# Transposing the features of two head pairs together, so that the w_in rows load in natural order

## The chip, the cores and the metric

The kernel runs on one core of one Trainium2 chip. The metric is the time of one execution in microseconds (us), as the median of several runs; shorter is better. The profile is of one such execution. Its span is about 2 us shorter than the timed value (212.5 against 214.5 us before). A run counts as slow when it is over 1.5% above the fastest run of the same kernel. The ratios, and the times that the text compares, are of the fast runs alone.

## The reference

Sliding-window attention (8 batches, 8 heads, 576 tokens, head size 64, window 32 each way), followed by a gated state-space layer. Cut to what matters:

```python
x    = attention(q, k, v)               # x[b, t, head * 64 + d]: the heads in order, 512 features
proj = x @ w_in                         # w_in: 512 x 1024
val, gate = proj[..., :512], proj[..., 512:]
for t in range(S):                      # a scan over the tokens
    h = exp(A_log) * h + val[:, t];  ys[:, t] = h
out  = (gate * sigmoid(gate) * ys) @ w_out
```

Any order of the 512 features between attention and projection is right, as long as the rows of `w_in` are in the same order.

## The kernel before

Tokens go in 9 chunks of 512 (8 blocks of 64). For each chunk and each of 4 head pairs TensorE (PE) makes scores (`sc`), ScalarE (ACT) the exponentials (`exp`), PE the product with v (`pv`), VectorE (DVE) the normalized result (`norm`) in 16 bit, and PE transposes it (`xt`), so that features lie on partitions; an eviction (`xe`) copies it from PSUM, where PE writes its results, to SBUF, from where it reads. Then come the projections (`pjv`, `pjg`), scan, gate, and output product (`fin`). Every engine follows an order written down in the kernel, one letter for each operation, and every load goes through the queue of the sync engine in the order of a list `ORDER`.

A head pair is heads 4G+s and 4G+2+s, because q and k are loaded in that arrangement. So each 128 features that come out of the transpose belong to two blocks of 64 rows of `w_in` that lie 128 rows apart. The load of `w_in` picks them:

```python
SLOTS = {..., "x16": 3, "xT": 2, ...}
        # loads
        elif kd == "ld" and key[0] == "a":
            nc.sync.dma_start(out=a_log, in_=moe_A_log.rearrange("(a p) -> p a", p=128))
            nc.scalar.activation(a1, a_log, AF.Exp, bias=0.0, scale=1.0)      # ACT, at the place of the load
        elif kd == "ld":
            _, i, a = key
            if i == 2:
                src = moe_w_out[128 * a:128 * a + 128, :]
            else:
                src = moe_w_in.rearrange("(g y s d) c -> g s y d c", g=2, y=2, s=2)[a // 2, a % 2, :, :, 512 * i:512 * i + 512]
            nc.sync.dma_start(out=bf("w32", i, a), in_=src)                   # 128 x 512 f32, 256 KB
        # ... (cut)
        elif kd == "cw":                                                      # cast to 16 bit
            i, a = key
            # ... (cut: w_out)
            copy(e, w_in16[:, a, 512 * i:512 * i + 512], bf("w32", i, a))
        # ... (cut)
        elif kd == "xt":                       # 4 transposes into free columns of the pv pair of banks
            x, pv = bf("x16", *key), bf("pv", *key)
            for half in range(2):
                dst = pv[:, half, 260:388].bitcast(f16)
                for r in range(2):
                    nc.tensor.transpose(out=dst[:, 128 * r:128 * r + 128],
                                        in_=x[:, 2 * half + r].rearrange("p h d -> p (h d)"), identity=ident)
        elif kd == "xe":                       # 36 evictions of 128 x 512
            c, hp = key
            copy(e, bf("xT", c)[:, hp, :].rearrange("p (a t) -> p a t", a=2),
                 bf("pv", *key)[:, :, 260:388].bitcast(f16))
```

The softmax here doesn't subtract the row's maximum and nothing guards it: scores larger than these inputs give would overflow.

Of the kernel before, what the change touches and what calls it, by code (L numbers as in the profile page):

```python
# [7 lines left out]
f32 = mybir.dt.float32  # L8
f16 = mybir.dt.float16
# [7 lines left out]

COST = {
    ("pe", "tr"): (0.50, 0.70), ("pe", "sc"): (0.235, 0.45), ("pe", "scm"): (0.455, 0.67), ("pe", "pv"): (0.265, 0.47),
    ("pe", "xt"): (0.23, 0.43), ("pe", "pj"): (0.864, 1.07), ("pe", "fin"): (0.864, 1.07),  # L20
    ("act", "ev"): (1.05, 1.20), ("act", "exp"): (0.92, 1.07), ("act", "tanh"): (0.50, 0.65),
    ("act", "fev"): (0.50, 0.65), ("act", "cv"): (0.53, 0.68), ("act", "cw"): (0.53, 0.68),
    ("act", "xe"): (0.50, 0.65), ("act", "sh"): (1.84, 1.99),
    ("dve", "ev"): (1.27, 1.40), ("dve", "mask"): (0.62, 0.74), ("dve", "rc"): (0.23, 0.25),
    ("dve", "norm"): (0.61, 0.74), ("dve", "xe"): (0.34, 0.47), ("dve", "scan"): (1.19, 1.33),
    ("dve", "silu"): (0.59, 0.72), ("dve", "cqk"): (0.66, 0.79),
    ("dve", "cv"): (0.34, 0.46), ("dve", "cw"): (0.34, 0.47), ("dve", "sh"): (0.62, 0.75),
    ("dve", "ar"): (0.65, 0.75), ("dve", "fuse"): (0.60, 0.72),
# [7 lines left out]
SWITCH, CAP, DLAT, DPRE = 0.095, 4.0, 0.95, 0.8  # L36
PEMASK = set(range(36))
SLOTS = {"stg": 5, "q16": 2, "k16": 2, "qT": 5, "kT": 5, "v32": 2, "vE": 2, "vO": 2, "pr": 3,
         "rc": 2, "x16": 3, "xT": 2, "f2k": 16, "th": 3, "si": 3, "fu": 2}
LETTER = {"L": "ld", "w": "cw", "a": "ar", "k": "ck", "K": "trk", "E": "evk", "q": "cq", "Q": "trq",  # L40
          "e": "evq", "v": "cv", "h": "sh", "S": "sc", "x": "exp", "P": "pv", "r": "rc", "n":
          "norm", "t": "xt", "T": "xe", "V": "pjv", "G": "pjg", "s": "scan", "g": "tanh", "u":
          "silu", "f": "fuse", "F": "fin", "o": "fev", "O": "out"}

SEQ = {
    "pe": "QQKSKSSPSPPPttQttKVVGSSGQVKVGSSPPPtPtGtQtKVGVVSSGQPPGtGKtVFSSFKPPFFttQKVGQQVSSSVGFKG"
          "PPSVttFSPPFGttQKFVVQGFSSSFPPGtVPPtGtFQGtVKQKVVSSKGQFSSPGFtKVKFPPPFtGtGtSSSVQGSPPGtFt"
          "VPPFGVKtFtGQVSSSFVGPPSGtVtSSPFVPPtVGtFGSSVFFtGFFPPPGtFtGVVVtVFGGVFVGVVFGGFFFFFFF",
    "act": "EvxvExxxwTTTTwgxgxeEvvgxxTTvTgeEghxxewggwwTgoxxEoooeEgexxxvgoEgxTTovxovgoeegoxxoxgTT"
           "ogvgeEEexxvgeoxxgoEEovoggxxxegxgoogToTexgxxogxTgTxxoTgoxgoxogooggooggogggoooooooo",  # L50
    "dve": "aqqeevvvhhrnrrwnrnneEsaususshhurnrnrnrnTsuuhssrnrTnuEusurrnnTTsuesshhurrnnusrrnnTTus"
           "EhuhsrnrnurnrTnsuTusssEhhurnTsurnrnTrnTTuhuhsrnrnuTTursnrunEsshuhsrnurnusrnrnssurTnu"
           "suTrrnnTurnTsuTssususssusuuf",
    "pool": "aakkqwkwwwwkqvfvvfqkfvvvvqfkfwfkfqkqqfvfvvvkfqkfqfqvvvfkkqffkqvvvfkkfvvqvvfqkffvfvvv"
            "fvfffffffffffff",
    "sp": "LLLLLLLLLLLLLLLLLLLLLLLLLLLLLLLLLLLLLLLLLLLLLLLLLLLLOLLLLLLLLLLLOOLLOLLLLLOLOLLLLOOL"
          "LLLLLLLOOOOLLOOOOOOOOOOOOOOOOOOOOOOOO",
}
SHARED = {
    "cw": "AGGDAGGGAAAG",  # L60
    "ar": "GDGD",
    "ck": "GGGGGGGGGGGGGGGG",
    "evk": "AADAADAAADAADAAD",
    "cq": "DDGGGGGGGGGGGGGG",
    "evq": "DDDAAAAADAAAAAAA",
    "cv": "DDAADGGGAAAGGGGGGAGGAAGGGAGAGGAGGGGGGGGG",
    "sh": "DDDDADDDDDDDDDDD",
    "xe": "AAAAAAADDADDAADDAADDDDDDDDAAAAADDDDD",
    "fuse": "GGGGGGGGGGGGGGGGGGGGGGGGGGGGGGGGGGGD",
}  # L70
ORDER = ["q01", "a", "v01", "q00", "v04", "k00", "v00", "v02", "k01", "v03", "w00", "w03",
         "q10", "k10", "w01", "w02", "w13", "w11", "w10", "w12", "k11", "q11", "v10", "v12",
         "v11", "v13", "v14", "k20", "q20", "v20", "v21", "v22", "v23", "v24", "q21", "w22",
         "k21", "w20", "w23", "w21", "k30", "q30", "k31", "q31", "v30", "q40", "v33", "v32",
         "v34", "v31", "k40", "v41", "v40", "q41", "k41", "q51", "v42", "q50", "k50", "v43",
         "k51", "v44", "v50", "q61", "q60", "v62", "v51", "k60", "v52", "v54", "v53", "k70",
         "v64", "k61", "v61", "v60", "v63", "v74", "q70", "v73", "q71", "v72", "k71", "v70",
         "v71"]
ORDER = [(x[0],) + tuple(int(y) for y in x[1:]) for x in ORDER]


# [8 lines left out]
def build(order):  # L90
# [3 lines left out]
    def add(kind, key, step, engs, cost, deps, new=(), use=()):  # L94
        o = Op()
        o.kind, o.key, o.engs, o.cost, o.deps = kind, key, engs, cost, [d for d in deps if d]
        o.new, o.use, o.step, o.n = list(new), list(use), step, len(ops)
        o.start = o.end = o.eng = None
        ops.append(o)
        last[(kind,) + key] = o  # L100
        return o
# [4 lines left out]
    g = last.get  # L106
    for it in order:
        if it[0] in "qk":
            add("ld", it, 0, ("sp",), 1.6, (), [("stg", it)])
        elif it[0] == "v":  # L110
            _, b, e = it
            add("ld", it, 0, ("sp",), 0.95 if e in (0, 4) else 1.24, (),
                [("v32", ("v32", b))])
        elif it[0] == "a":
            add("ld", it, 0, ("sp",), 0.8, ())
        else:
            add("ld", it, 0, ("sp",), 0.7, (), [("f2k", ("w32",) + it[1:])])
# [19 lines left out]
    for c in range(NCH):  # L137
        bs = sorted({(8 * c + r) // NBLK for r in range(8)})
        for hp in range(HP):
            k, st = (c, hp), 4 * c + hp  # L140
            s = add("sc", k, st, ("pe",), "scm" if st in PEMASK else "sc", [g(("ev" + n, b, hp // 2)) for n in "qk" for b in bs],
                    [("ps2", ("sc",) + k)], [(n + "T", b, hp // 2) for n in "qk" for b in bs])
            x = add("exp", k, st, ("act",), "exp", [s], [("pr", ("pr",) + k)], [("sc",) + k])
            m = x if st in PEMASK else add("mask", k, st, ("dve",), "mask", [x], (), [("pr",) + k])
            p = add("pv", k, st, ("pe",), "pv", [m] + [g(("cv", b, e)) for b in bs for e in range(5)] +
                    [g(("sh", b, i)) for b in bs for i in range(2)],
                    [("ps2", ("pv",) + k)], [("pr",) + k] + [(n, b) for n in ("vE", "vO") for b in bs])
            r = add("rc", k, st, ("dve",), "rc", [p], [("rc", ("rc",) + k)], [("pv",) + k])
            r = add("norm", k, st, ("dve",), "norm", [r], [("x16", ("x16",) + k)], [("pv",) + k, ("rc",) + k])
            t = add("xt", k, st, ("pe",), "xt", [r], (), [("x16",) + k, ("pv",) + k])  # L150
            add("xe", k, st, ("dve", "act"), "xe", [t], [("xT", ("xT", c))], [("pv",) + k])
    for c in range(NCH):
        xs = [g(("xe", c, hp)) for hp in range(HP)]
        for cc in range(4):
            k, st = (c, cc), 4 * c + cc
            pv = add("pjv", k, st, ("pe",), "pj", xs + [g(("cw", 0, a)) for a in range(4)],
# [121 lines left out]
def kernel(  # L278
# [18 lines left out]
    def T(shape, dt, tag):  # L297
# [2 lines left out]
    SHAPES = {"stg": ([128, 2, 9, 64], f32), "q16": ([128, 9, 2, 64], f16), "k16": ([128, 9, 2, 64], f16),  # L300
              "qT": ([128, 2, 576], f16), "kT": ([128, 2, 640], f16), "v32": ([128, 5, H, D], f32),
              "vE": ([128, 5, H, 65], f16), "vO": ([128, 4, H, 65], f16), "pr": ([128, 2, 512], f16),
              "rc": ([128, 4, 2], f32), "x16": ([128, 4, 2, 64], f16), "xT": ([128, HP, 512], f16),
              "f2k": ([128, 512], f32), "th": ([128, 512], f16), "si": ([128, 512], f16), "fu": ([128, 4, 512], f16)}
    bufs = {p: [T(SHAPES[p][0], SHAPES[p][1], f"{p}_{i}") for i in range(n)] for p, n in SLOTS.items() if p != "f2k"}
    f2k = T([128, SLOTS["f2k"], 512], f32, "f2k")
# [60 lines left out]
    def emit(o):  # L367
        e, key = o.eng, o.key

        def bf(*k):  # L370
            p, i = place[o.n, k]
            if p == "ps1":
                return psum[:, i, :]
            if p == "ps2":
                return psum[:, i:i + 2, :]
            return bufs[p][i]
# [16 lines left out]
        elif kd == "ld":  # L393
            _, i, a = key
            if i == 2:
                src = moe_w_out[128 * a:128 * a + 128, :]
            else:
                src = moe_w_in.rearrange("(g y s d) c -> g s y d c", g=2, y=2, s=2)[a // 2, a % 2, :, :, 512 * i:512 * i + 512]
            nc.sync.dma_start(out=bf("w32", i, a), in_=src)  # L399
        elif kd == "cw":  # L400
            i, a = key
# [70 lines left out]
            nc.vector.reciprocal(bf("rc", *key), view[:, :, :, 64])  # L472
        elif kd == "norm":
            view = bf("pv", *key)[:, :, 0:260].rearrange("p h (r x) -> p r h x", x=65)
            nc.vector.tensor_tensor(out=bf("x16", *key), in0=view[:, :, :, 0:64],  # L475
                                    in1=bf("rc", *key)[:, :, :, None].to_broadcast([128, 4, 2, 64]), op=ALU.mult)
        elif kd == "xt":
            x, pv = bf("x16", *key), bf("pv", *key)
            for half in range(2):
                dst = pv[:, half, 260:388].bitcast(f16)  # L480
                for r in range(2):
                    nc.tensor.transpose(out=dst[:, 128 * r:128 * r + 128],  # L482
                                        in_=x[:, 2 * half + r].rearrange("p h d -> p (h d)"), identity=ident)
        elif kd == "xe":
            c, hp = key
            copy(e, bf("xT", c)[:, hp, :].rearrange("p (a t) -> p a t", a=2),
                 bf("pv", *key)[:, :, 260:388].bitcast(f16))
        elif kd in ("pjv", "pjg"):
            c, cc = key
            oc = cc if kd == "pjv" else 4 + cc  # L490
# [63 lines left out]
```

## Time and profile before

| | before |
|---|---|
| time, median of all its runs in the first result | 214.59 us (212.74 to 215.18) |
| span of the profiled run | 212.5 us |
| PE busy | 162.1 us (76%) |
| DVE, ACT, POOL busy | 135.1, 120.8, 101.8 us |
| bytes moved by DMA | 41.22 MB |

The shares hide two stages. The table of stretches shows them. Its columns are: the stretch, its length, busy time and number of instructions of each engine, the granted PE clock, the DMA share (1.00 would be all 16 DMA engines busy; it adds up the times of packets, and can come out a little above 1), and GB/s.

```profile
core 0: us, PE busy (x) PEld busy (x) DVE busy (x) ACT busy (x) POOL busy (x), PEclk, DMA share, GB/s
20.00:30.00 10.00, 4.41 (x108) 3.56 (x104) 3.81 (x10) 3.73 (x5) 1.15 (x1) 0.84 0.30 99
30.00:40.00 10.00, 3.00 (x18) 1.59 (x17) 2.61 (x2) 1.08 (x2) 2.35 (x3) 0.50 0.13 51
40.00:50.00 10.00, 2.37 (x6) 0.60 (x4) 1.86 (x3) 0.00 (x0) 0.62 (x1) 0.50 0.13 51
50.00:60.00 10.00, 1.03 (x2) 0.13 (x2) 0.00 (x0) 0.63 (x1) 0.00 (x0) 0.50 0.73 193
61.00:209.00 148.00, 143.95 (x1872) 81.58 (x1872) 116.81 (x173) 108.11 (x151) 88.53 (x90) 0.99 0.75 218
```

From 30 to 50 us every engine is nearly idle, and so is DMA, at 0.13 of its engines: 2 of 16. From 61 us on PE is busy 97% of the time. What all wait for in between is in the chain of waits (start, length, what):

```profile
18.04 1.28 SPq L399
19.36 5.72 SPq L399
25.12 3.53 SPq L399
28.70 7.16 SPq L399
35.90 5.00 SPq L399
40.95 19.42 DMA f2k<-in_moe_w_in_dram
60.44 0.63 POOL w_in L358
61.11 1.19 PE psum L493 x2
```

SPq is the queue of the sync engine, L399 the issue of a weight load, L493 a projection. The queue is held by the issues of `w_in` loads, then the last of these takes 19.4 us to land, and only then the first full projection can end. The timeline of the sync engine has the `w_in` loads beside the loads of `w_out`, which have the same size and natural row order:

```profile
18.04 27.91 SPq L399 DMA_DIRECT2D f2k<-in_moe_w_in_dram  x6
...
76.72 1.41 SPq L399 DMA_DIRECT2D f2k<-in_moe_w_out_dram  x3
```

Six issues took 27.9 us here and three took 1.4 us there. The groups that the change touches (line, engine, operation, shapes, count, busy us, mean ns, idle time before and what ended it):

```profile
L482 PE MATMUL psum<-ident,x 128*128 128x128 f16 x144 | 14.0, 227 | 4.3 <-DVE x L475 4.2
L351 ACT ACTIVATE xT<-psum 128x512 f16<-128x512 f16 x17 | 9.9, 596 | 10.5 <-PE psum L482 10.2
L354 DVE COPY xT<-psum 128x512 f16<-128x512 f16 x19 | 7.7, 418 | 4.9 <-PE psum L482 4.8
```

### The profile page before, as it was taken

Reading aid. Unit: us, or ns where it says so; the run is one execution under the profiler, and the core shown is the slowest. Engines: PE = TensorE matmul, PEld = TensorE weight load, DVE = VectorE, ACT = ScalarE, POOL = GpSimd, SP = SyncE. Lnnn points to the kernel's source line nnn. Section 1 sums busy time; section 2 is a strip of 40 time slices with the busy share of each in tenths; the row PEclk is TensorE's granted clock in tenths of the full one; section 3 lists DMA queues with packets and bytes.
Section 4 is the critical chain, followed back from the end, with each engine's and each line's share of the span. In section 5 each row is a group of like instructions: output and inputs, shape, how many; then the busy total and the mean of one; then the engine's idle time right before and its main releaser. Section 6 shows DMA issues by size and latency. Waiting matters only on the chain.

```text
span 212.5 us, 5136 instructions
## 1 busy us (share of the span) xinstructions
PE 162.1 (76%) x2088; PEld 93.1 (44%) x2088; DVE 135.1 (64%) x218; ACT 120.8 (57%) x167; POOL 101.8 (48%) x115
## 2 busy tenths in 40 slices
PE   0258242500149798999999999899899999999993
PEld 0235132100025555576565566566555564554441
DVE  5463250500016969948876988958988977688950
ACT  2038330000118799888995959986737875733273
POOL 6440023101058469788568847475975424206430
PEclk9999955555559999999999999999999999999998
DMA  6997211113858999999999979999971111321145
GB/s 155 304 221 200 95 51 51 51 52 92 233 134 235 256 252 354 362 234 256 305 352 285 344 186 265 313 241 307 358 263 54 49 52 52 146 92 61 49 170 224
DMA packets 53558, 41.22 MB, mean 194 GB/s; under 512 B 39200, under 2 KB 39200, under 8 KB 53536
## 3 DMA queue, kind: packets, MB, share of 16 engines
q1 hardware_dynamic: 53536, 40.90, 66.6%
q8 instruction: 16, 0.26, 0.5%
q14 instruction: 6, 0.05, 0.1%
HBM read 31.46 MB, written 9.44 MB: 192 GB/s over the span
## 4 chain that ended last, share of the span: by engine, by line
PE 55%; DMA 12%; SPq 12%; DVE 7%; ACT 7%; issue 3%; POOL 2%; DVEq 0%; ACTq 0%; POOLq 0%
PE psum L493 24%; PE psum L513 14%; SPq L399 11%; DMA f2k<-in_moe_w_in_dram 9%; PE psum L420 5%; PE psum L468 4%; PE psum L446 3%; DMA stg<-in_k_dram 3%; PE psum L482 3%; DVE vO L354 3%; PE psum L451 3%; ACT kT L351 2%; DVE f2k L498 2%; ACT pr L455 2%; ACT qT L351 1%
## 5 line engine op out<-in xcount | busy, mean ns | idle before, releaser
L493 PE MATMUL psum<-xT,w_in 128*128 128x512 f16 x288 | 73.8, 390 | 21.0 <-ACT w_in L351 13.1
L508 POOL TENSOR_TENSOR fu<-f2k,si 128x512 f16<-128x512 f32 x35 | 42.3, 1210 | 33.9 <-DVE f2k L498 17.7
L493 PEld LDWEIGHTS <-w_in 128*128 128x128 f16 x288 | 26.4, 99 | 49.3 <-ACT w_in L351 14.0
L498 DVE TENSOR_TENSOR_SCAN f2k<-arep,f2k,psum 128x512 f32<-128x512 f32 x32 | 40.2, 1271 | 7.5 <-PE psum L493 6.8
L503 DVE SCALAR_TENSOR_TENSOR si<-th,psum 128x512 f16<-128x512 f16 x36 | 24.4, 681 | 26.9 <-ACT th L501 24.9
L455 ACT ACTIVATE pr<-psum 128x1024 f16<-128x1024 f32 x36 | 35.6, 1025 | 5.3 <-PE psum L451 4.1
L513 PE MATMUL psum<-w_out,fu 128*128 128x512 f16 x144 | 35.6, 379 | 0.0
L501 ACT ACTIVATE th<-psum 128x512 f16<-128x512 f32 x36 | 21.4, 597 | 18.5 <-PE psum L493 17.9
L351 ACT ACTIVATE f2k<-psum 128x512 f32<-128x512 f32 x36 | 21.5, 600 | 16.2 <-PE psum L513 15.4
L358 POOL TENSOR_SCALAR q<-stg 128x1152 f16<-128x1152 f32 x14 | 16.6, 1184 | 24.4 <-DMA stg<-in_q_dram 23.6
L475 DVE TENSOR_TENSOR x<-psum,rc 128x512 f16<-128x512 f32 x36 | 24.1, 681 | 0.7
L358 POOL TENSOR_SCALAR k<-stg 128x1152 f16<-128x1152 f32 x16 | 18.4, 1152 | 9.2 <-DMA stg<-in_k_dram 9.1
L420 PE MATMUL psum<-ident,q 128*128 128x128 f16 x144 | 11.9, 236 | 10.6 <-DVE q L354 9.1
L513 PEld LDWEIGHTS <-fu 128*128 128x128 f16 x144 | 13.1, 97 | 13.5 <-issue 0.3
L358 POOL TENSOR_SCALAR vE<-v 128x512 f16<-128x512 f32 x26 | 15.9, 627 | 4.5 <-DMA v<-in_v_dram 2.6
L420 PE MATMUL psum<-ident,k 128*128 128x128 f16 x144 | 12.1, 236 | 7.4 <-POOL k L358 6.0
L351 ACT ACTIVATE kT<-psum 128x1152 f16<-128x1152 f16 x11 | 12.4, 1140 | 9.2 <-PE psum L420 9.1
L482 PE MATMUL psum<-ident,x 128*128 128x128 f16 x144 | 14.0, 227 | 4.3 <-DVE x L475 4.2
L358 POOL TENSOR_SCALAR w_in<-f2k 128x512 f16<-128x512 f32 x5 | 3.1, 619 | 28.9 <-DMA f2k<-in_moe_w_in_dram 28.9
L451 PEld LDWEIGHTS <-kT 64*128 64x128 f16 x576 | 14.0, 100 | 5.0 <-issue 1.3
L446 PE MATMUL psum<-eye,madd 64*128 64x512 f16 x72 | 15.0, 413 | 1.5 <-ACT kT L351 1.5
L351 ACT ACTIVATE xT<-psum 128x512 f16<-128x512 f16 x17 | 9.9, 596 | 10.5 <-PE psum L482 10.2
(48 smaller groups left out, 174.3 us busy)
## 6 DMA issues: line engine op xcount, KB each, us to landing
stg<-in_q_dram SPq DMA_DIRECT2D x16, 576.0 KB, 10.9
stg<-in_k_dram SPq DMA_DIRECT2D x16, 576.0 KB, 8.1
out_dram<-f2k SPq DMA_DIRECT2D x36, 256.0 KB, 2.4
v<-in_v_dram SPq DMA_DIRECT2D x24, 256.0 KB, 8.6
v<-in_v_dram SPq DMA_DIRECT2D x16, 192.0 KB, 6.4
f2k<-in_moe_w_in_dram SPq DMA_DIRECT2D x8, 256.0 KB
f2k<-in_moe_w_out_dram SPq DMA_DIRECT2D x4, 256.0 KB, 6.7
a_log<-in_moe_A_log_dram SPq DMA_DIRECT2D x1, 2.0 KB
```

The source lines that it names most:

```text
L351: nc.scalar.activation(dst, src, AF.Copy, bias=0.0, scale=mul)
L358: nc.gpsimd.tensor_scalar(out=dst, in0=src, scalar1=mul, scalar2=1.0, op0=ALU.mult, op1=ALU.mult)
L399: nc.sync.dma_start(out=bf("w32", i, a), in_=src)
L420: nc.tensor.transpose(out=t[:, 128 * j:128 * j + 128], in_=s[:, j].rearrange("p y d -> p (y d)"), identity=ident)
L455: nc.scalar.activation(bf("pr", *key), bf("sc", *key), AF.Exp, bias=0.0, scale=1.0 / 8.0)
L475: nc.vector.tensor_tensor(out=bf("x16", *key), in0=view[:, :, :, 0:64], in1=bf("rc", *key)[:, :, :, None].to_broadcast([128, 4, 2, 64]), o ...
L493: nc.tensor.matmul(out=pj, lhsT=w_in16[:, fc, 128 * oc:128 * oc + 128], rhs=xT[:, fc, :], start=(fc == 0), stop=(fc == 3))
L498: nc.vector.tensor_tensor_scan(out=bf("h", *key), data0=arep[:, cc, 512 - 64 * c:1024 - 64 * c], data1=bf("pjv", *key), initial=init, op0= ...
L501: nc.scalar.activation(bf("th", *key), bf("pjg", *key), AF.Tanh, bias=0.0, scale=0.5)
L503: nc.vector.scalar_tensor_tensor(out=bf("si", *key), in0=bf("th", *key), scalar=1.0, in1=bf("pjg", *key), op0=ALU.add, op1=ALU.mult)
L508: eng.tensor_tensor(out=bf("fu", c)[:, cc, :], in0=bf("h", *key), in1=bf("si", *key), op=ALU.mult)
L513: nc.tensor.matmul(out=fo, lhsT=fu[:, cc, 128 * tt:128 * tt + 128], rhs=w_out16[:, cc, :], start=(cc == 0), stop=(cc == 3))
```

## The change

The intent: `norm` writes two head pairs into one token tile in which the heads stand in natural order. Once both are there, eight transposes go into one PSUM bank of their own, and one eviction of 128x1024 takes them out. The features then have natural order, and the `w_in` load takes 128 rows as they lie. The orders of all engines and the order of the loads were made anew. Cut to its core:

```diff
-         "rc": 2, "x16": 3, "xT": 2, ...
+         "rc": 2, "x16": 2, "xT": 2, ...
 SEQ = { ... the order of every engine: all new (cut) ... }
-ORDER = ["q01", "a", "v01", "q00", "v04", "k00", "v00", "v02", "k01", "v03", "w00", "w03", "q10", ...
+ORDER = ["q01", "k01", "k00", "q00", "v00", "v03", "v01", "v02", "w01", "v04", "w03", "w11",
+         "k10", "q10", "w00", "w10", "w02", "a", "w13", "w12", ...
@@ build
-            t = add("xt", k, st, ("pe",), "xt", [r], (), [("x16",) + k, ("pv",) + k])
-            add("xe", k, st, ("dve", "act"), "xe", [t], [("xT", ("xT", c))], [("pv",) + k])
+            if hp % 2:
+                kg = (c, hp // 2)
+                t = add("xt", kg, st, ("pe",), "xt", [r, g(("norm", c, hp - 1))], [("ps1", ("xt",) + kg)], [("x16",) + kg])
+                add("xe", kg, st, ("dve", "act"), "xe", [t], [("xT", ("xT", c))], [("xt",) + kg])
@@ load
-                src = moe_w_in.rearrange("(g y s d) c -> g s y d c", g=2, y=2, s=2)[a // 2, a % 2, :, :, 512 * i:512 * i + 512]
+                src = moe_w_in[128 * a:128 * a + 128, 512 * i:512 * i + 512]
@@ xt, xe
-            for half in range(2):
-                dst = pv[:, half, 260:388].bitcast(f16)
-                for r in range(2):
-                    nc.tensor.transpose(out=dst[:, 128 * r:128 * r + 128], ...
+            x, t = bf("x16", *key), bf("xt", *key).bitcast(f16)
+            for a in range(2):
+                for r in range(4):
+                    nc.tensor.transpose(out=t[:, 512 * a + 128 * r:512 * a + 128 * r + 128],
+                                        in_=x[:, r, 2 * a:2 * a + 2].rearrange("p h d -> p (h d)"), identity=ident)
-            copy(e, bf("xT", c)[:, hp, :]..., bf("pv", *key)[:, :, 260:388].bitcast(f16))
+            copy(e, bf("xT", c)[:, 2 * G:2 * G + 2, :].rearrange("p a t -> p (a t)"), bf("xt", *key).bitcast(f16))
```

In `ORDER`, "w0a" and "w1a" are the val and gate halves of the rows of tile a, and "a" is `A_log`. The new list moves "k01" from the eighth to the second place, "a" from the second to the 18th, and "w00" from the 10th to the 15th.

## The prediction

> **What bounds the kernel now.** Until 61 us, the weight loads. In the table of stretches TensorE is busy 1.0 to 3.0 us of each 10 us between 30 and 60 us, and DMA runs at 51 GB/s with a share of 0.13, which is 2 of 16 engines. The chain of waits has the sync queue held in issuing w_in loads (18.0 to 41 us), then one w_in transfer (40.9 to 60.4 us). The w_out loads, equal in bytes but in natural row order, issue in 0.4 us (median) against 4.3 us. The cause, by the Trainium skill, "DMA: Bandwidth & Descriptors", section "Why a DMA increments its semaphore by 16 and not by 1": the number of engines is the largest up to 16 that divides the slowest dimension of both patterns; here the source's is y = 2, so 2. The 0.13 share agrees. From 61 to 209 us TensorE bounds: busy 143.95 of 148 us at clock 0.99; DMA is near full too (share 0.93 to 1.07 between 60 and 140 us) but ends its loads by 157 us.
>
> **What the change does.**
> 1. The w_in source becomes 128 rows: 16 engines. 2.1 MB at the 230 to 300 GB/s of full slices is 7 to 9 us, not 41 (at 51 GB/s), and the loads behind are not blocked. Nearly all is on the critical path.
> 2. xt: the same 144 transposes, by eights in an own bank; no change on PE.
> 3. xe: 36 evictions of 128x512 (596 ns on ACT, 418 on DVE: 18 us) become 18 of 128x1024 (exp's 1025 ns for 1024 columns on ACT, an estimated 0.7 us on DVE: 15 us), on engines that don't bound: about 0.
> 4. xt takes a bank from the projections, but pv's pair is freed earlier: within 1 us.
> 5. All engines' orders are made anew: noise, 2 us either way.
>
> **Time.** Before w02, which the first full projection needs, the new order loads six q/k (3.54 MB), v of batch 0 (1.18) and six w_in (1.57): 6.3 MB. At about 255 GB/s from 2.3 us on, it lands at 27 us; cast and start: 28 us instead of 61. PE will have done by then what it had done before at 61 us, except ten projection matmuls (2.2 us). The rest takes 148 + 2.2 us, the tail (last eviction, store) 3.5 us: span 181.5. The timed value is 2 us above the span: **182 us, 8 in 10 within 176 to 188.** Faster by over 2%: 0.98; within 2%: 0.015; slower: 0.005.
>
> **What would show it.** Step 1: w_in issues of about 0.5 us; no stretch at 51 GB/s; DMA share near 1 from 5 to 30 us; no wait for w_in over 5 us; first run of four projection matmuls at 26 to 30 us. Step 2: 144 transposes, equal busy time. Step 3: 18 xT copies, ACT near 1.02 us, DVE 0.65 to 0.8 us. Steps 4 and 5: PE busy over 94% from 35 us to 4 us before the end.
>
> **What would make it wrong.** Loads of batches 1 and 2 (an estimated 13 us of DMA a batch, 16 us of PE a chunk) starve PE between 30 and 60 us: up to 190. The new order packs PE tighter than the 12 us of gaps, switches and slow clock that 61 to 209 us still holds (an estimated 136 us of pure warm PE work in 148): down to 174.

## The result, and the profile after

| | before | after |
|---|---|---|
| time, median | 214.59 us (4 runs) | 186.23 us (184.93 to 187.53, 4 runs) |
| ratio of fast runs | | 0.8691 (95% interval 0.861 to 0.8772) |
| span of the profiled run | 212.5 us | 184.5 us |
| first run of projections starts | 61.1 us | 30.8 us |
| PE busy | 162.1 us (76%) | 155.5 us (84%) |

A ratio is the mean time of a kernel's fast runs over the mean of the other's fast runs of the same rounds, so it is not quite the ratio of the medians.

The table of stretches after, with the same columns:

```profile
0.00:10.00 10.00, 0.00 (x0) 0.00 (x0) 2.83 (x20) 1.28 (x1) 3.64 (x14) 1.00 0.85 264
10.00:20.00 10.00, 6.13 (x124) 5.31 (x124) 5.78 (x9) 4.20 (x4) 3.60 (x5) 1.00 1.10 276
20.00:30.00 10.00, 4.16 (x70) 3.83 (x71) 4.54 (x9) 5.59 (x9) 6.61 (x7) 0.66 1.10 329
30.00:40.00 10.00, 9.58 (x98) 5.36 (x96) 9.62 (x16) 6.96 (x11) 4.54 (x6) 1.00 1.02 328
31.00:181.00 150.00, 144.18 (x1882) 81.61 (x1880) 119.80 (x171) 109.66 (x148) 85.86 (x84) 1.00 0.72 211
```

The stretches at 51 GB/s are gone; DMA is full from 10 to 40 us. The stage after the first projection is as long as before: 150 us for 288 projection matmuls where it was 148 us for 278. But PE is still idle for half of 20 to 30 us. The chain of waits after, up to the first projections (L494; L457 is the exponential of the scores, L470 the product with v, L422 the transposes of q and k, L484 those of the features, L356 an eviction):

```profile
17.06 7.06 DMA a_log<-in_moe_A_log_dram
24.25 2.84 ACT pr L457 x3
27.14 0.66 PE psum L470 x16
27.80 1.07 PE psum L422 x9
28.87 0.85 PE psum L484 x8
29.72 0.69 PE psum L422 x9
30.90 0.70 DVE xT L356
31.64 4.06 PE psum L494 x18
```

No `w_in` load stands in it. In its place stands the load of `A_log`, 2 KB. The timeline of ACT shows why:

```profile
17.96 1.02 ACT L457 ACTIVATE pr<-psum 128x1024 f16<-128x1024 f32 x1
24.14 0.20 ACT L394 ACTIVATE a<-a_log 128x4 f32<-128x4 f32 x1 [5.16 <-DMA a_log<-in_moe_A_log_dram]
24.25 2.83 ACT L457 ACTIVATE pr<-psum 128x1024 f16<-128x1024 f32 x3
```

The exponential of `A_log` (L394) stands in ACT's order between the first and the second score exponential (L457) of chunk 0. It waited 5.2 us for its load, which had moved from the second to the 18th place and was now issued behind 17 others, and the other three score exponentials, whose scores had long been made, waited with it. The timeline of the sync engine:

```profile
14.78 1.95 SPq L401 DMA_DIRECT2D f2k<-in_moe_w_in_dram  x3
17.06 0.38 SPq L393 DMA_DIRECT2D a_log<-in_moe_A_log_dram  x1
17.48 1.66 SPq L401 DMA_DIRECT2D f2k<-in_moe_w_in_dram  x2
```

Three `w_in` issues take 2 us here. The groups that the change touched:

```profile
L484 PE MATMUL psum<-ident,x 128*128 128x128 f16 x144 | 11.5, 225 | 0.0
L353 ACT ACTIVATE xT<-psum 128x1024 f16<-128x1024 f16 x8 | 8.2, 1022 | 3.6 <-PE psum L484 2.4 <-DVE f2k L499 1.1
L356 DVE COPY xT<-psum 128x1024 f16<-128x1024 f16 x10 | 6.8, 684 | 4.0 <-PE psum L484 3.9
```

The transposes take the same time each (225 against 227 ns), and the evictions fell from 17.6 to 15.0 us in sum.

### The profile page after: what moved, and what is told of

It is laid out like the page before. It is cut to its first block, busy times and chain, and to the rows that moved or that the text cites. A ratio compares the mean times of both kernels' runs of the same rounds, so it can differ in the third digit from the quotient of the medians.

```text
span 184.5 us, 5094 instructions
## 1 busy us (share of the span) xinstructions
PE 155.5 (84%) x2088; PEld 91.6 (50%) x2088; DVE 133.8 (73%) x209; ACT 122.3 (66%) x163; POOL 99.7 (54%) x110
## 4 chain that ended last, share of the span: by engine, by line
PE 50%; DMA 18%; SPq 11%; ACT 8%; POOL 5%; DVE 4%; issue 1%; POOLq 0%; ACTq 0%; DVEq 0%
PE psum L494 21%; PE psum L514 13%; DMA v<-in_v_dram 7%; SPq L390 6%; DMA out_dram<-f2k 5%; PE psum L422 5%; ACT pr L457 4%; DMA a_log<-in_moe_A_log_dram 4%; PE psum L470 4%; SPq L384 3%; PE psum L448 3%; DMA stg<-in_q_dram 3%; PE psum L484 3%; PE psum L453 3%; POOL k L360 2%; ACT qT L353 2%
## 5 line engine op out<-in xcount | busy, mean ns | idle before, releaser
L494 PE MATMUL psum<-xT,w_in 128*128 128x512 f16 x288 | 68.9, 380 | 0.2 <-DVE xT L356 0.2
L509 POOL TENSOR_TENSOR fu<-f2k,si 128x512 f16<-128x512 f32 x35 | 43.7, 1260 | 36.9 <-DVE si L504 36.1
L494 PEld LDWEIGHTS <-w_in 128*128 128x128 f16 x288 | 26.4, 98 | 27.5 <-issue 0.7
L457 ACT ACTIVATE pr<-psum 128x1024 f16<-128x1024 f32 x36 | 35.6, 1027 | 3.6 <-PE psum L453 2.4
L360 POOL TENSOR_SCALAR vE<-v 128x512 f16<-128x512 f32 x28 | 17.0, 621 | 26.3 <-DMA v<-in_v_dram 26.3
L353 ACT ACTIVATE qT<-psum 128x1152 f16<-128x1152 f16 x14 | 15.8, 1137 | 15.3 <-PE psum L422 15.3
L422 PE MATMUL psum<-ident,q 128*128 128x128 f16 x144 | 11.9, 234 | 14.5 <-DVE q L356 12.8
L470 PE MATMUL psum<-vE,pr 128*64 128x65 f16 x320 | 13.9, 201 | 7.1 <-ACT pr L457 6.2
L422 PEld LDWEIGHTS <-q 128*128 128x128 f16 x144 | 9.9, 106 | 17.0 <-DVE q L356 12.8
L470 PEld LDWEIGHTS <-pr 128*64 128x64 f16 x576 | 11.5, 115 | 13.1 <-ACT pr L457 6.6
L353 ACT ACTIVATE kT<-psum 128x1152 f16<-128x1152 f16 x12 | 13.6, 1137 | 4.2 <-PE psum L422 4.2
L474 DVE RECIPROCAL rc<-psum 128x8 f32<-128x8 f32 x36 | 7.2, 200 | 12.5 <-PE psum L470 12.4
L453 PEld LDWEIGHTS <-kT 64*128 64x128 f16 x576 | 12.7, 95 | 4.1
```

What stands on the lines that cost most here:

```text
L353: nc.scalar.activation(dst, src, AF.Copy, bias=0.0, scale=mul)
L360: nc.gpsimd.tensor_scalar(out=dst, in0=src, scalar1=mul, scalar2=1.0, op0=ALU.mult, op1=ALU.mult)
L422: nc.tensor.transpose(out=t[:, 128 * j:128 * j + 128], in_=s[:, j].rearrange("p y d -> p (y d)"), identity=ident)
L457: nc.scalar.activation(bf("pr", *key), bf("sc", *key), AF.Exp, bias=0.0, scale=1.0 / 8.0)
L470: nc.tensor.matmul(out=pv[p0:p0 + 64, h, 65 * (r // 2):65 * (r // 2) + 65], lhsT=pr[:, h, 64 * r:64 * r + 64], rhs=vt, start=True, stop=True)
L494: nc.tensor.matmul(out=pj, lhsT=w_in16[:, fc, 128 * oc:128 * oc + 128], rhs=xT[:, fc, :], start=(fc == 0), stop=(fc == 3))
```

## The experiments

Two questions: is the load the whole gain, and if so by what mechanism; and where did the last 4 us against the prediction go? The table has the changed kernel and the eleven kernels that were made to find out. "Wrong" means wrong on purpose. Where a kernel had slow runs, the median of the fast ones differs from that of all.

| kernel | result | us, median of all runs (range) | us, median of fast runs | ratio of fast runs to before (95% interval) |
|---|---|---|---|---|
| changed kernel | correct | 186.23 (184.93 to 187.53) | 186.23 | 0.8691 (0.861 to 0.8772) |
| b_natural | wrong | 178.59 (178.18 to 180.35) | 178.59 | 0.8323 (0.8266 to 0.8381) |
| a_oldload | wrong | 215.86 (215.56 to 217.04) | 215.86 | 1.0037 (0.9982 to 1.0092) |
| b_two64 | correct | 184.14 (183.24 to 185.16) | 184.14 | 0.8568 (0.8516 to 0.8619) |
| a_oldorder | correct | 181.61 (181.32 to 183.48) | 181.61 | 0.8467 (0.841 to 0.8524) |
| b_ownbank | wrong | 180.55 (179.06 to 182.03) | 180.45 | 0.8418 (0.8378 to 0.8457) |
| a_afirst | correct | 183.19 (181.82 to 185.3) | 182.82 | 0.8533 (0.8469 to 0.8596) |
| a_qfirst | correct | 185.69 (184.35 to 187.27) | 185.62 | 0.865 (0.8588 to 0.8712) |
| a_both | correct | 182.12 (181.64 to 183.18) | 182.12 | 0.8511 (0.8459 to 0.8563) |
| b_shift | correct | 183.32 (180.95 to 186.18) | 182.44 | 0.8511 (0.8461 to 0.856) |
| b_wide | correct | 188.70 (186.15 to 190.94) | 187.52 | 0.8751 (0.8696 to 0.8806) |
| b_wide_alt | correct | 186.12 (183.63 to 187.45) | 184.50 | 0.8659 (0.8612 to 0.8706) |

### b_natural: the load alone

```diff
 (kernel before)
-                src = moe_w_in.rearrange("(g y s d) c -> g s y d c", ...)[a // 2, a % 2, :, :, 512 * i:512 * i + 512]
+                src = moe_w_in[128 * a:128 * a + 128, 512 * i:512 * i + 512]
```

> The kernel before with the w_in source alone made natural (128 rows in order); everything else old, so the features and weight rows do not match and the result is wrong on purpose. Theory E (the number of DMA engines that one w_in load uses, 2 against 16, is the whole gain): w_in issues of about 0.5 us, no stretch at 51 GB/s, time 180 to 188 us, within 3% of the changed kernel (186). Rival S (the regrouped transposes and the new engine orders bring a good part of it): 195 us or more.

Measured: 178.6 us, under the expected 180 to 188. The projections start at 25.7 us. The load alone is worth 36 us (214.5 less 178.6), more than the whole change, which brought 28 us. So the rest of the change costs time.

### a_oldload: the change without its load

```diff
 (changed kernel)
-                src = moe_w_in[128 * a:128 * a + 128, 512 * i:512 * i + 512]
+                src = moe_w_in.rearrange("(g y s d) c -> g s y d c", ...)[a // 2, a % 2, :, :, 512 * i:512 * i + 512]
```

> The changed kernel with the old w_in source alone put back (wrong result on purpose: weight rows do not match the features). Theory E: the 51 GB/s stretches return, V of chunk 0 starts at about 60 us, time 211 to 220 us. Rival S: it keeps a part of the gain, under 205 us.

Measured: 215.9 us, the same as before within the interval. The stretch from 30 to 40 us is again at 51 GB/s with PE idle:

```profile
30.00:40.00 10.00, 0.00 (x0) 0.00 (x0) 0.00 (x0) 0.00 (x0) 2.30 (x2) 0.50 0.13 51
```

Theory E holds from both sides; rival S falls.

### b_two64: the same permuted rows over all engines

```diff
 (kernel before, load of w_in)
+                for y in range(2):
+                    r0 = 256 * (a // 2) + 128 * y + 64 * (a % 2)
+                    nc.sync.dma_start(out=bf("w32", i, a)[64 * y:64 * y + 64],
+                                      in_=moe_w_in[r0:r0 + 64, 512 * i:512 * i + 512])
```

> The kernel before with each w_in load issued as two loads of 64 rows into the halves of the same tile: same rows, same permuted order, correct result, but the slowest dimension is 64 and not 2. Theory E: as fast as b_natural to within 3 us (eight more issues of about 0.5 us on the queue), 181 to 190 us, each half over all 16 engines. Rival R (it is the row order, blocks of 64 rows taken from 128 rows apart, that is slow in memory): still 51 GB/s and about 212 to 216 us.

Measured: 184.1 us, within the expected 181 to 190, but 5.5 us slower than b_natural and not within 3. The rows are as far apart in memory as before, yet 51 GB/s is gone: it was the number of engines, not the row order, and rival R falls. The remaining 5.5 us were not expected. To compare the rates, one needs a stretch in which nothing but `w_in` was loaded. The packet sizes in the traces show where that is (2304 bytes in q and k loads, 256 in v loads, 2048 in these `w_in` loads). In b_natural it is 20 to 22 us:

```profile
20.00:22.00 2.00, 2.00 (x76) 1.56 (x70) 0.90 (x2) 1.48 (x3) 1.31 (x2) 1.00 1.06 407
```

In b_two64 it is 20 to 23 us:

```profile
20.00:23.00 3.00, 2.45 (x91) 2.01 (x86) 2.19 (x6) 2.56 (x3) 1.40 (x3) 1.00 1.05 283
```

The engines are as busy (share 1.05) but move 283 GB/s instead of 407. The last twelve issues also took 10.1 us in the queue, where six took 3.9 us in b_natural, so that the next k and q loads started at 25.0 us instead of 18.6 us. The first projections were not late for it: they start at 25.4 us, against 25.7 us in b_natural. The time was lost behind them: from there to the last eviction b_two64 took 153.0 us and b_natural 146.9. From 30 to 40 us PE was busy 6.5 us against 8.3 us, and the chain of waits leads there through the late issues of v loads and a v load that landed at 37.5 us. So the trace puts the loss on what waited in the queue behind the half loads; no run tests that alone. Whether the count of issues or the halved tiles did it was open; b_wide was made to tell.

### b_wide and b_wide_alt: half the partitions, full width

```diff
 (kernel before, load of w_in: 64 rows of all 1024 columns, into two tiles)
+                r0 = 256 * (a // 2) + 128 * i + 64 * (a % 2)
+                i0, i1 = place[o.n, ("w32", 0, a)][1], place[o.n, ("w32", 1, a)][1]
+                nc.sync.dma_start(out=f2k[64 * i:64 * i + 64, i0:i1 + 1:i1 - i0, :],
+                                  in_=moe_w_in[r0:r0 + 64, :].rearrange("d (i c) -> d i c", i=2))
```

> The kernel before with its features, its orders and its row permutation, but each w_in load takes 64 rows of all 1024 columns (slowest dimension 64, 256 KB, eight loads as before) where it took two blocks of 64 rows of 512 columns. Correct result. Theory E: 16 engines; unlike the sixteen loads of b_two64 (184.1) it needs no more issues, so it comes to b_natural (178.6) within about 2 us: 178 to 181 us, the fastest correct version. The projections of val need now all eight loads and not four: up to 1.5 us later than b_natural's 25.7 us. Rival R (permuted blocks are slow in memory): over 185 us.

Measured: 187.5 us in the fast runs (188.7 over all), 6.5 us over the range that I expected of theory E, and inside the range that I had given to rival R. But rival R can't be the reason: 64 rows of all 1024 columns are one unbroken block of 256 KB in memory. And the count of issues is the same as in b_natural, so it was not the issues alone. The first projections start at 34.1 us. All engines are busy again, and the rate is lower still, here from 23 to 27 us, where again only `w_in` was loaded (its packets have 4096 bytes in this kernel; the profile is of a slow run):

```profile
23.00:27.00 4.00, 0.78 (x20) 0.56 (x20) 0.26 (x2) 0.21 (x1) 0.00 (x0) 0.77 1.05 228
```

The Trainium skill has this on the page "SBUF — State Buffer", section "Door 1: The DMA port swizzle": partitions 0 to 63 reach 8 of the 16 ports through which DMA writes, measured there at 196 GB/s against 328 GB/s for all 128. The rates here are both higher, 228 against 407 GB/s, but about as far apart in ratio. In b_wide the first four `w_in` loads all write partitions 0 to 63. A later section of the page, "Can I just issue two DMAs to hit both halves?", says no: two such transfers came to 6% more than one. b_wide_alt tests that, with the halves alternating:

```diff
 (b_wide)
-ORDER = [..., "w00", "w03", "q10", "k10", "w01", "w02", "w13", "w11", "w10", "w12", ...
+ORDER = [..., "w00", "w10", "q10", "k10", "w03", "w13", "w01", "w11", "w02", "w12", ...
```

> b_wide came out at 188.7 us, not 178 to 181: its w_in loads used all engines (share 1.05) but 14 to 22 us moved 268 GB/s where b_natural moved 362 to 401. In b_wide the first four loads all write partitions 0 to 63 and the last four 64 to 127; this kernel only alternates the halves in the queue. Theory P (the write side of half the partitions is what limits, and two loads to both halves in flight share it out): 330 GB/s or more while w_in loads, first projection at 26 to 29 us, 179 to 183 us. Rival Q (each load to 64 partitions is slow by itself and loads do not help each other, as the Trainium skill's page on SBUF says of two such transfers): w_in still at 220 to 300 GB/s, first projection after 32 us, 186 to 190 us.

Measured: 184.5 us in the fast runs (186.1 over all), the first projections at 30.7 us, and from 22 to 26 us, with `w_in` alone,

```profile
22.00:26.00 4.00, 1.88 (x60) 1.46 (x54) 1.26 (x5) 2.14 (x3) 0.00 (x0) 1.00 1.06 244
```

244 against 228 GB/s is 7% more, close to the 6% of the page, though one of the two profiles is of a slow run. The 330 GB/s of theory P did not come, and the rate is in the range of rival Q. The time and the start of the projections lie between the two expectations: in its fast runs b_wide_alt is 3 us faster than b_wide, so alternating gained something. How much it can gain is open: b_two64, which alternates halves with loads of half the size, moved 283 GB/s. None of the three comes near 407. So a natural-order load is fast for two reasons: 128 rows spread over 16 engines, and all 128 partitions are written by one transfer (b_two64 has the row length of b_natural, b_wide and b_wide_alt its number of loads; what all three have and b_natural does not are loads of 64 rows into 64 partitions). That the write ports are the reason is the page's statement; the runs show the rates, and none tells 64 partitions from 64 rows in a load.

### a_oldorder and b_ownbank: what the regrouping costs

a_oldorder is the changed kernel with the old orders:

```diff
 (changed kernel)
-SEQ, SHARED, ORDER = (the new orders)
+SEQ, SHARED, ORDER = (the old orders; of each two "t" in PE's order and each two "T" the first is left out)
```

> The changed kernel (regrouped transposes in an own bank, natural rows, correct result) with the orders of the kernel before on all engines, out of which only the first transpose group and the first eviction of each pair are taken. Against b_natural it differs by the regrouping alone. Theory E: regrouping is worth nothing on the critical path, within 2 us of b_natural. Rival S: faster than b_natural by over 3 us. If the own bank costs projections, slower by 1 to 3 us. Also, its load of A_log comes second as before, so the 5.2 us wait of ACT for A_log seen in the changed kernel should be absent.

Measured: 181.6 us, correct. Against b_natural (178.6), from which it differs by the regrouping alone, it is 3.0 us slower: regrouping is not free, at least with orders that were not made for it. Against the changed kernel (186.2), from which it differs by the orders alone, it is 4.6 us faster. It has the lowest median of all correct kernels, though its interval overlaps those of a_both, b_shift, a_afirst and, by a hair, b_two64. As expected, ACT's wait for `A_log` is gone. The end of the start-up in its chain of waits (L447 is the normalization, L453 the transposes of the features, L463 a projection):

```profile
24.39 1.16 DVE x L447 x2
...
25.59 0.63 PE psum L453 x8
...
26.25 1.03 ACT xT L322
...
27.32 2.75 PE psum L463 x12
```

In b_natural the same place reads (L420 are transposes of q and k, L482 of the features, L493 is a projection):

```profile
24.82 0.47 PE psum L482 x8
25.29 0.50 PE psum L420 x9
25.79 2.69 PE psum L493 x12
```

With the regrouping the first projection waits for two normalizations, then eight transposes, then an eviction of 1.03 us, and starts 1.6 us later (27.3 against 25.7), of which 0.3 us were there when the first k load on the chain landed (11.3 us against 11.1). In b_natural the evictions were short and PE had other work behind them. From there to the last eviction a_oldorder took 150.6 us and b_natural 146.9, but the profiled run of a_oldorder was its slowest (183.5, with a median of 181.6), so a part of that is not the kernel's.

b_ownbank takes one part of the regrouping into b_natural:

```diff
 (b_natural)
-            t = add("xt", k, st, ("pe",), "xt", [r], (), [("x16",) + k, ("pv",) + k])
+            t = add("xt", k, st, ("pe",), "xt", [r], [("ps1", ("xt",) + k)], [("x16",) + k])
 (the four transposes and the eviction use that bank)
```

> The kernel b_natural (178.6 us, wrong result on purpose, old orders) with one part of the regrouping: each of the 36 transposes-of-features goes to a bank of its own instead of the free columns of its pv pair; still four transposes and one 128x512 eviction each. It splits the 3.0 us by which a_oldorder (181.6) is slower than b_natural. Theory B (the extra bank taken from the projections costs it): 180.5 to 182 us. Rival G (the grouping costs it: two head pairs must both be normalized before any of the two is transposed, and one longer eviction follows): within 1 us of 178.6.

Measured: 180.5 us, 1.9 us slower than b_natural, with intervals that just overlap (0.8266 to 0.8381 and 0.8378 to 0.8457). By the time theory B fits. The profile does not bear it out: from the first projection to the last eviction it took 146.9 us (27.8 to 174.7), just as b_natural did. It only started 2.1 us later, and 1.2 us of that were there before any feature was transposed: the first k load on the chain landed at 12.3 us and not at 11.1 us. So a cost of the bank is not shown. The start of the kernel varies by about that much between runs, and this pair can't settle it.

### a_afirst, a_qfirst and a_both: the new start-up wait

```diff
 (changed kernel; a_afirst)
-ORDER = ["q01", "k01", ..., "w02", "a", "w13", ...
+ORDER = ["q01", "a", "k01", ..., "w02", "w13", ...
```

> The changed kernel with the A_log load moved from the 18th to the second place of the queue, as the kernel before had it. Theory A (the exp of A_log stands in ACT's order at the place of its load, waits 5.2 us there and holds back three score exponentials of chunk 0, and so the first projection, 30.8 us instead of the predicted 28): ACT's wait after the first exp of chunk 0 falls from 5.2 us to under 1 us, the first projection starts at 26 to 29 us, time 2 to 4 us under the changed kernel: 182 to 184. Rival W (the weights or the loads of batch 0 would hold the first projection to 30 us anyway): within 1 us of it.

```diff
 (changed kernel; a_qfirst)
-    "dve": "vqkqehhr...
+    "dve": "qkqvehhr...
```

> The changed kernel with the first DVE cast of v (which waits 6.7 us for its load) put after the casts of q, k, q. Theory: PE's first transpose moves from 12.8 us to about 9 us, but by theory A the exponentials then still wait for A_log until 24.1 us, so the first projection stays at 30 to 31 us and the time within 1 us of the changed kernel. Rival: the start of PE sets the rest, 3 us faster.

a_both has both edits.

> Both edits together. Theory A: first projection set by the last w_in rows (landing about 25 to 26 us) and the evictions, 26 to 28 us; time 181 to 184 us, 2.5 to 5 us under the changed kernel and at least as fast as the A_log edit alone. Rival W: no better than the changed kernel by more than 1 us.

Measured, in the fast runs: a_afirst 182.8 us, 3.4 us faster than the changed kernel, as theory A expected; its first two projection matmuls start at 25.9 us and the run of projections at 27.0 us. (Its profile fell in the slow state, by its time; the starts are quoted with that reservation.) a_qfirst 185.6 us, within 1 us of the changed kernel as expected, so it is the wait for `A_log` that counts. But the reason that I gave for a_qfirst was partly wrong: the first transpose came at 11.0 us and not at 9 us. With v out of the way DVE waited for q itself. The timeline of DVE in a_both:

```profile
11.88 0.76 DVE L356 CAST q<-stg 128x1152 f16<-128x1152 f32 x1 [6.97 <-DMA stg<-in_q_dram]
```

In the kernel before, the first q landed in time for a cast at 8.3 us; the new load order issues four q and k loads one after the other, and they seem to land together (that was not tested). a_both came to 182.1 us, with the run of projections from 26.9 us. The timeline of its ACT shows the four exponentials in one piece:

```profile
19.40 3.77 ACT L457 ACTIVATE pr<-psum 128x1024 f16<-128x1024 f32 x4
```

The four end at 23.2 us where they had ended at 27.1 us. Of the 4.6 us that the new orders cost, these two edits give back 4.1.

### b_shift: natural rows, features left as they were

```diff
 (kernel before, natural load; the cast puts the rows in place)
-                copy(e, w_in16[:, a, 512 * i:512 * i + 512], bf("w32", i, a))
+                for y in range(2):
+                    copy(e, w_in16[64 * y:64 * y + 64, a, 512 * i:512 * i + 512],
+                         bf("w32", i, 2 * (a // 2) + y)[64 * (a % 2):64 * (a % 2) + 64])
```

> The kernel before with natural w_in rows and the features left as they were: the cast to 16 bit of each w_in tile becomes two half casts of 64 partitions that put the rows where the features want them (from two loaded tiles), so the result is correct without regrouping. Eight extra half casts of about 0.6 us on ACT, POOL and DVE in the first 28 us, spread over three engines. If the load was all that had to be mended and the regrouping is what costs 3 us: 178.5 to 181 us, faster than the changed kernel (186.2), than a_oldorder (181.6) and than both start-up edits (182.1). If the extra casts hold the first projection: it starts at 28 us or later and the time is 181 to 184.

Measured: 182.4 us in the fast runs (180.95 to 183.63), correct. By the median it is the second of the two expectations. The profile, which is of a slow run, has the projections from 28.9 us, and DVE doing two casts of 64x512 (0.73 and 0.88 us) ahead of a normalization that PE then waited for. A half cast on ACT took 622 ns where a whole one took 627 in the kernel before, so halving the partitions saved nothing.

## Why the prediction was right, and where its steps were off

The predicted time was 182 us (176 to 188), the measured one 186.2. The range held and the main step was right, but the time is 4.2 us above the centre and some of the steps fell.

1. "The w_in source becomes 128 rows: 16 engines. [...] Nearly all is on the critical path." Right. Issues took 0.59 us (median) where 0.5 was predicted, DMA share was 1.10 from 10 to 30 us, and no engine waited over 5 us for `w_in`. b_natural and a_oldload show that the load is the whole gain, and more: 36 us with the old orders and features (214.5 less 178.6), 30 us with the new ones (215.9 less 186.2).
2. "xt: the same 144 transposes [...] no change on PE." Right: 225 ns against 227 ns each.
3. The evictions were predicted at 15 us in sum, 0.7 us each on DVE, and came to 15.0 us and 0.684 us. "Engines that don't bound: about 0" holds for the busy time. It left out that regrouping makes the first head pair of two wait for the second.
4. "xt takes a bank from the projections, but pv's pair is freed earlier: within 1 us." With step 3 this puts the whole regrouping at about 1 us, and that fell: it costs 3.0 us on the old orders, which were not made for it (a_oldorder against b_natural). In the one pair of profiles 1.3 us of that arise between the first k load and the first projection, where two normalizations and a longer eviction stand in the way; starts vary by about as much between runs (see b_ownbank), so this share is an indication only. The bank itself may cost nothing: the projections and all after them took 146.9 us with the own bank and without it.
5. "All engines' orders are made anew: noise, 2 us either way." This step fell. The new orders cost 4.6 us (186.2 against 181.6), of which 4.1 are the start-up waits. I had looked for what the new load order brings earlier and not for what it brings later: the 2 KB of `A_log` went from the second to the 18th place, and ACT, which takes its work in order, waited for it. The wait is visible in the diff once one asks which engine reads each load, and at what place in its order.
6. The sum. It put the first projections at 28 us, what follows at 148 + 2.2 us and the tail at 3.5 us. Measured were 30.8 us, 150.2 us (30.84 to 181.01) and 3.5 us (184.5 less 181.0). So the mis-sized term is the start, 2.8 us short (and outside the 26 to 30 us that the prediction had named), and its cause is step 5: with the wait removed, projections run from 26.9 us (a_both). What I had taken to set it, the landing of `w_in` at 27 us, did not: in the changed kernel the last packet of all eight `w_in` loads had ended by 25.0 us. That a_both comes near 28 us is in part luck. The other 1.5 us are my own arithmetic: a span of 181.5 plus 2 is 183.5, not the 182 that the text gives.
7. "PE busy over 94% from 35 us to 4 us before the end." Right: 139.98 of 145.5 us, 96%. The fear that loads of batches 1 and 2 would starve PE did not come true: the stage is as long as predicted.

What stays open: how the 3.0 us of regrouping divide, whether the bank has a part in them, and why the stage after the first projections is shorter in b_natural and b_ownbank (146.9 us) than in the kernels with grouped features (150 us and more). Grouping alone is not shown to be the reason: b_shift, with ungrouped features, took 151.7 us there, in a slow run.

## What to carry to other kernels

When a load is slow, look at the DMA share in its stretch: 0.13 at 51 GB/s said "2 of 16 engines" before any experiment, and a pattern whose slowest dimension is 2 was the reason; then load with one transfer over all 128 partitions, because two transfers of 64 came off worse here even with all engines busy (228 to 283 GB/s against 407). When a queue is reordered, ask for each load that moved later which engine waits for it in order, and what stands behind it: 2 KB held back three exponentials by some 4 us here. And measure the parts of a change apart: here one line was worth more than the whole (b_natural, though its result is wrong), and putting the old orders back gave a correct kernel (181.6 us) faster than the changed one (186.2 us).

## What the Trainium skill lacked or had wrong

- "DMA: Bandwidth & Descriptors", section "Why a DMA increments its semaphore by 16 and not by 1": its rule for the number of engines agrees with these runs (slowest dimension 2: 51 GB/s at a share of 0.13; 64 or 128: a share of about 1). I found nothing there on what a load on 2 engines does to the loads queued behind it: here six issues held the sync queue for 27.9 us, and from 30 to 50 us the DMA share was 0.13, as much as 2 of 16 engines.
- "SBUF — State Buffer", sections "Door 1: The DMA port swizzle" and "Can I just issue two DMAs to hit both halves?": both agree in kind (with only `w_in` loads under way, 407 GB/s to 128 partitions, 228 to one half after the other, 244, 7% more, with alternating halves). The figures of the first section, 196 and 328 GB/s for a transfer of 1 MiB, are lower than these, which are for queues of 256 KB loads. And 283 GB/s in b_two64, whose loads alternate too but have half the size, is 24% over the 228, more than the second section's 6% would give. The DMA share does not show these differences: it was 1.05 to 1.06 in all four.
- I found no page with the time that a small load takes behind large ones: the 2 KB of `A_log` took 7.1 us from issue to landing in the 18th place of the queue and 4.4 us in the second (a_afirst).
- "TensorE: Matmul & The Clock Gate", section "Part 1: The HAM clock gate", has the clock at half after idle time, and that agrees: in the idle stretch of the kernel before it was 0.50, and in that of the changed kernel, 20 to 30 us, 0.66 on average.
